# Softmax-weighted 7-tap convolution into a two-layer FFN on one core: the first block's transposed taps in two PSUM banks, and a new order of work

## The chip, the cores and the metric

One core of a Trainium2 chip runs the whole program. The metric is the device time of one execution in microseconds; lower is better. The number shown for a kernel is the median of its runs.

## The reference

For x of (4, 4096, 192) and weight_gen of (4, 4096, 8, 7), all float32:

```python
w = softmax(weight_gen, axis=-1)              # per position and head, over 7 taps
x_pad = x with 6 zero rows in front           # along the sequence
a[b, s, h, g] = sum_k w[b, s, h, k] * x_pad[b, s + k, h, g]     # 8 heads of 24 columns
u = a.reshape(16384, 192) @ w_in              # 192 x 2048
g = u * sigmoid(1.702 * u)
out = g @ w_out                               # 2048 x 192
```

The sigmoid is computed as a tanh: g = u/2 * (1 + tanh(0.851 u)).

## The kernel before, in words

The 16,384 positions are cut into 32 blocks of 512. A block's FFN is 16 units: a unit (block, f) is one [128 x 512] tile of u, that is 128 of the 2,048 hidden columns for 512 positions. Units are counted through, 0 to 15 for block 0, 16 to 31 for block 1, and so on.

**The order is written by hand.** `ORDER` (line 37) is a string of actions, one after the other, and `act` (line 755) issues the instructions of each. Since each engine and each DMA queue works through its own instructions in the order of issue, the string sets the order on every engine; semaphores between engines follow from the data. `ORDER` reaches to unit 101. From there `PERIOD` (line 22) is repeated for two blocks at a time; the change doesn't touch it.

**Block 0 is special** (`SWAP = 1`, line 383). Its products are taken in float32, since the weights are not yet split into two float16 parts by the time it starts:

- `s0.n`: the softmax of its weights (line 204).
- `ta.k` (`first_tap`, line 267): VectorE multiplies x, shifted by k, with tap k's weights, for the first 128 columns and a bit; `sum.k.l` (line 285) adds two taps on VectorE. `tb.k` and `tb.kp` (lines 301, 311) do the last 64 columns on POOL: tap by tap, then sums ("rests").
- `tr.k` (`turn_tap`, line 288): four TensorE products with the identity transpose a tap and add it in PSUM; `trb.k` (line 317) the same for the rests.
- `ka.n` (`keep_a`, line 390): copies of the two halves of the turned block to SBUF, ka.0 by ScalarE (line 396), ka.1 by VectorE (line 394). `kb.n` (line 398) are four copies of the rests, two by each (lines 405, 407).
- `W.f` (`whole`, line 541): 128 of 192 rows of the first product for unit f. `X.n` (`halves`, line 546): the remaining 64 rows, for units 4n to 4n + 3, two of them at a time in the two halves of the array. A unit is complete with both.
- `S.f` (`second`, line 577): the second product of unit f, four 128x192 pieces (`a` and `b`: two of them).
- `warm.n` (line 718): n matmuls of no use in front of all that; their result is never read.

**The weights** arrive as int64 words and are reduced in place, piece by piece: `nb` and `nm` on ScalarE, `n1` and `n2` on VectorE (line 470). Later `na`, `bin`, `bout` find their largest magnitude, and `ph`, `pl`, `ps` split them in two float16 parts (line 517); `mv` moves parts to the other half of the partitions by DMA.

**Blocks from 1 on**: softmax `s`, then `a` (`attend`, line 249): seven products and six sums on POOL. `c` (line 358) finds the block's scale with a product of one column on TensorE ("top", line 348) in the middle, `x` (line 409) splits in two float16 parts, `tu` transposes them by DMA, and `xd` copies them crosswise to the other half of the partitions, into the tile xd for odd blocks and into room in rt for even ones (line 420). `P.n` (`pair`, line 597) is the first product of units 2n and 2n + 1, 18 matmuls. P.8 is the first of block 1, P.16 the first of block 2. `gt`, `gm` (line 553) are the gate: tanh on ScalarE, a product on VectorE; `gh`, `gl` (line 570) split the result on the same two, and with them the unit's PSUM bank comes free. `U` (line 622) and `C` (line 639) are the second product, for 128 and for 64 output columns.

**PSUM**: units take the banks h0 to h3 in turn (unit mod 4, line 537). A pool tag names a bank; the turned block is in h1, the rests in h3, the second product of block 0 in o0 and o1. The scheduler puts a wait between two engines that use the same tile.

Of the kernel before, what the change touches and what calls it, by code (L numbers as in the profile page):

```python
# [38 lines left out]
tr.3 tb.1p ta.1 ta.5 tb.2 nm.t0 tb.3 sum.0.1 tb.3p nb.t0 tb.5 s1.0 trb.0 s1.1 tr.5 s1.2 n1.i0 n2.i0 s1.3 n1.t0
s1.4 tb.4 nb.i1 tb.5p tr.2 s1.5 nm.i1 n2.t0 tb.6 trb.2 s1.6 tr.0 tb.6p ka.1 ka.0 a1.0 nm.o0 W.1 a1.1 trb.4 a1.1p  # L40
kb.1 W.2 kb.0 kb.2 kb.3 n1.i1 n2.i1 W.0 X.0 nb.t1 nb.o0w n1.o0 W.3 gt.0 gt.1 nm.o1 gm.0 n2.o0 gt.2 nm.i2 a1.2
gm.1 W.4 n1.o1 a1.2p a1.3 gt.3 S.0b nb.i2w gm.2 gm.3 S.0a n2.o1 a1.3p nb.o2w W.5 X.1 W.7 W.6 n1.i2 n2.i2 s2.0
S.3 nm.i3 gt.4 s2.1 n1.i3 n2.i3 nm.t1 s3.0 a1.4 gm.4 n1.t1 nb.o4w gt.5 gm.5 a1.4p gt.7 s2.2 n2.t1 W.8 a1.5 nm.o2
W.9 n1.o2 a1.5p gt.6 s2.3 na.i2w gm.6 s2.4 nm.o4 n2.o2 gm.7 nm.o3 n1.o3 na.i0w S.2 X.2 s2.5 n2.o3 gt.8 gm.8
n1.o4 gt.9 s2.6 a1.6 gm.9 a1.6p W.10 a2.0 na.t0w W.11 n2.o4 W.12 gt.11 bin.0 W.13 a2.1 gm.11 S.4 gt.10 gm.10
na.o2w bin.1 c1.0 bin.2 S.9 na.o0w c1.1 c1.2 lp2 s5.0 a2.1p x1.0 X.3 S.6 x1.1 W.15 nm.o5 ph.i2w x1.2 s3.1 n1.o5
tu1 ph.i0w cg1 n2.o5 W.14 pl.i0w a2.2 na.o4w S.8 S.1a bout.0 gt.13 bout.1 S.10 mv.0 gm.13 a2.2p gt.14 bout.2
S.1b ph.t0w gm.14 gt.12 s5.1 pl.t0w xd1 s3.2 a2.3 ph.o4w gm.12 S.11 ph.o0w S.14b P.8 a2.3p gt.15 s5.2 gm.15
pl.i2w ph.o2w gt.17 a2.4 a2.4p s5.3 s4.0 P.9 s5.4 gt.16 gm.17 gh.17 gt.18 gm.16 gl.17 ps.o0w s3.3 gt.19 S.13
pl.o2w gm.18 gh.16 S.7 a2.5 gl.16 s3.4 gh.18 gm.19 gh.19 gl.18 s4.1 S.14a ps.o4w gl.19 S.15b P.10 s3.5 a2.5p  # L50
gt.20 P.11 pl.o0w S.5 gm.20 gt.21 gm.21 S.15a pl.o4w gh.21 gt.22 gh.20 S.12 gt.23 gl.21 a2.6 mv.1 gm.22 gl.20
U.16 gh.22 s4.2 P.12 s3.6 gm.23 ps.o2w a2.6p st.0a st.0b c2.0 gh.23 gt.24 c2.1 gl.22 s5.5 U.20 gl.23 a3.0 c2.2
x2.0 gm.24 U.18 s4.3 gt.25 x2.1 gh.24 U.21 gm.25 a3.1 gh.25 P.13 gt.26 U.17 gl.24 x2.2 U.22 gl.25 gt.27 gm.26
gm.27 U.23 P.14 a3.1p gh.26 cg2 U.24 gh.27 gl.26 gt.29 tu2 gl.27 gt.28 a3.2 co1 gm.29 gh.29 P.15 s4.4 a3.2p
gm.28 gl.29 gh.28 a3.3 U.19 gl.28 gt.31 gm.31 xd2 a3.3p U.26 gt.30 gh.31 gm.30 U.25 gh.30 gl.31 P.16 gt.32 U.31
s4.5 gl.30 gm.32 P.17 gt.33 a3.4 gm.33 U.27 a3.4p gh.32 gh.33 gt.34 s4.6 gt.35 gl.32 U.28 a3.5 gl.33 gm.34 a3.5p
a3.6 P.18 gm.35 gh.34 gl.34 a3.6p gh.35 gt.37 gt.36 gl.35 U.29 gm.37 U.30 gh.37 gm.36 c3.0 U.32 gh.36 P.19 stU.1
# [882 lines left out]
```

## Time and profile before

| | us |
|---|---|
| median of 3 runs | 1036.33 |
| lowest, highest | 1035.56, 1036.49 |
| the profiled execution | 1035.99 |
| its span | 1034.2 |
| TensorE busy in it | 1028.2 |
| VectorE, ScalarE, POOL busy | 849.6, 718.2, 729.6 |

The span is the time from the first to the last instruction of the execution that the profiler recorded; some 1.8 us of the execution lie around it. Matmuls are pipelined, so that of one can overlap the next; the start of the next says more than the duration. A float32 matmul is recorded as two rows (two passes).

### The profile page before, as it was taken

Reading aid. Unit: us, or ns where it says so; the run is one execution under the profiler, and the core shown is the slowest. Engines: PE = TensorE matmul, PEld = TensorE weight load, DVE = VectorE, ACT = ScalarE, POOL = GpSimd, SP = SyncE. Lnnn points to the kernel's source line nnn. Section 1 sums busy time; section 2 is a strip of 40 time slices with the busy share of each in tenths; the row PEclk is TensorE's granted clock in tenths of the full one; section 3 lists DMA queues with packets and bytes.
Section 4 is the critical chain, followed back from the end, with each engine's and each line's share of the span. In section 5 each row is a group of like instructions: output and inputs, shape, how many; then the busy total and the mean of one; then the engine's idle time right before and its main releaser. Section 6 shows DMA issues by size and latency. Waiting matters only on the chain.

```text
span 1034.2 us, 23101 instructions
## 1 busy us (share of the span) xinstructions
PE 1028.2 (99%) x9251; PEld 583.1 (56%) x9251; DVE 849.6 (82%) x1606; ACT 718.2 (69%) x1211; POOL 729.6 (71%) x497
## 2 busy tenths in 40 slices
...
GB/s 352 110 36 94 52 81 56 58 109 16 99 42 60 88 26 99 52 97 48 33 103 38 100 42 47 99 27 99 52 67 79 25 105 37 42 42 47 37 27 21
DMA packets 70771, 70.93 MB, mean 69 GB/s; under 512 B 51660, under 2 KB 57164, under 8 KB 69256
## 3 DMA queue, kind: packets, MB, share of 16 engines
...
q14 instruction: 35, 0.29, 0.1%
...
## 4 chain that ended last, share of the span: by engine, by line
PE 97%; DVE 1%; ACT 0%; DMA 0%; issue 0%; DVEq 0%
PE h L615 47%; PE o L634 31%; PE o L647 16%; PE o L587 2%; PE h L544 1%; PE h L550 1%; DVE tap L280 0%; DMA rt<-xt 0%; DVE row L151 0%; ACT bits L479 0%; DVE m L496 0%; PE o L672 0%; PE rest L672 0%; PE top L348 0%; DVE x L407 0%
## 5 line engine op out<-in xcount | busy, mean ns | idle before, releaser
L556 ACT ACTIVATE th<-h,s 128x512 f32<-128x512 f32 x496 | 317.0, 684 | 131.4 <-PE h L615 112.1
L561 DVE SCALAR_TENSOR_TENSOR h<-th,h 128x512 f32<-128x512 f32 x496 | 324.0, 690 | 69.2 <-ACT th L556 66.6
L261 POOL TENSOR_TENSOR acc<-acc,prod 128x768 f32<-128x768 f32 x186 | 339.4, 1825 | 13.0
L245 POOL TENSOR_TENSOR prod<-xb,wb 128x768 f32<-128x768 f32 x186 | 294.3, 1582 | 10.7
L615 PE MATMUL h<-xt,w0h 64*128 64x512 f16 x992 | 205.3, 376 | 0.0
L615 PE MATMUL h<-xt,th 64*128 64x512 f16 x496 | 183.1, 376 | 0.0
L615 PE MATMUL h<-xd,moved 64*128 64x512 f16 x768 | 156.5, 376 | 0.0
L615 PE MATMUL h<-rt,moved 64*128 64x512 f16 x720 | 149.9, 376 | 0.2 <-DMA rt<-xt 0.2
L229 POOL TENSOR_TENSOR wb<-wb,wr 128x224 f32<-128x224 f32 x31 | 18.9, 608 | 174.6 <-DVE wr L223 158.1
L615 PEld LDWEIGHTS <-moved 64*128 64x128 f16 x1488 | 96.0, 94 | 66.5
L575 DVE SCALAR_TENSOR_TENSOR g<-g,h 128x512 f16<-128x512 f16 x184 | 120.4, 681 | 7.8 <-ACT g L573 4.2
L573 ACT ACTIVATE g<-h 128x512 f16<-128x512 f32 x184 | 109.4, 597 | 25.0 <-DVE h L561 23.9
L575 DVE SCALAR_TENSOR_TENSOR ro<-ro,h 128x512 f16<-128x512 f16 x156 | 102.0, 681 | 7.3 <-ACT ro L573 4.2
L573 ACT ACTIVATE ro<-h 128x512 f16<-128x512 f32 x156 | 92.8, 597 | 20.0 <-DVE h L561 19.1
L615 PE MATMUL h<-xt,w0l 64*128 64x512 f16 x496 | 104.0, 376 | 0.0
L615 PE MATMUL h<-xd,th 64*128 64x512 f16 x256 | 96.3, 376 | 0.0
L615 PE MATMUL h<-xt,tl 64*128 64x512 f16 x248 | 93.2, 376 | 0.0
L693 ACT ACTIVATE osl<-o,s 64x512 f32<-64x512 f32 x31 | 21.1, 682 | 100.8 <-PE o L647 100.8
L615 PEld LDWEIGHTS <-w0h 64*128 64x128 f16 x992 | 63.9, 94 | 47.0 <-issue 1.4
L634 PEld LDWEIGHTS <-wos 64*128 64x128 f16 x984 | 64.0, 94 | 46.6 <-issue 0.4
L615 PE MATMUL h<-rt,th 64*128 64x512 f16 x240 | 90.2, 376 | 0.0
L615 PEld LDWEIGHTS <-th 64*128 64x128 f16 x992 | 64.1, 94 | 46.0
...
## 6 DMA issues: line engine op xcount, KB each, us to landing
...
xd<-xt SPq DMA_DIRECT2D x32, 192.0 KB, 2.9
rt<-xt SPq DMA_DIRECT2D x30, 192.0 KB, 2.9
...
```

Of the source, the lines that this page charges most:

```text
L229: eng.tensor_tensor(w, w, r, ALU.mult)
L245: eng.tensor_tensor(to.rearrange("p j (h g) -> p (j h) g", g=G), xv, wv, ALU.mult)
L261: nc.gpsimd.tensor_tensor(acc, acc, t, ALU.add)
L556: nc.scalar.activation(t, hp[u], AF.Tanh, scale=scale[u[0]][:, 4:5] if u[0] else SIG / 2)
L561: nc.vector.scalar_tensor_tensor(to, th.pop(u), 1.0, hp[u], ALU.add, ALU.mult)
L573: nc.scalar.activation(g[:, 0], hp[u], AF.Copy, scale=2.0**-12)
L575: nc.vector.scalar_tensor_tensor(g[:, 1], g[:, 0], -(2.0**12), hp.pop(u), ALU.mult, ALU.add)
L587: nc.tensor.matmul(o, lhsT=g[:, s], rhs=w, start=a and j % 2 == 0, stop=z, skip_group_check=True)
L615: nc.tensor.matmul(to, lhsT=w, rhs=x, start=i == 0, stop=i == last)
L634: nc.tensor.matmul(po[blk, e], lhsT=w[h, f * D : f * D + P], rhs=g[h, i], start=first and i == 1, stop=w is woh and n == NF - (4 if blk == ...
L647: nc.tensor.matmul(po[blk, 2][h * C1 : (h + 1) * C1], lhsT=w[:, d + P : d + D], rhs=gg[blk, f + h][:, i], start=f == 0 and i == 1, stop=f ...
L693: nc.scalar.activation(t, po[blk, 2][far_], AF.Copy, scale=s[far_, 5:6])
```

## The change

It touches four places.

- `warm`: 12 spare matmuls instead of 19.
- `turn_tap` writes the four transposed pieces of a tap into two banks, h1 and o0, two in each; `keep_a` copies one half from each. The rests go to o1 instead of h3 (`turn_rest`).
- `X.n` is now two actions, `X.na` and `X.nb`, for two units each.
- `ORDER` is written anew from its first action to unit 101.

Of the order's 46 lines the first is shown.

```diff
--- before.py
+++ after.py
@@ -35,52 +35,52 @@
...
-warm.19 s0.0 ident s0.1 s0.2 s0.3 s0.4 s0.5 s0.6 nb.i0 s0.7 nm.i0 ta.0 ta.4 tb.0 tr.4 ta.6 tr.6 ta.3 ta.2 tb.1
...
+warm.12 s0.0 s0.1 s0.2 s0.3 s0.4 s0.5 s0.6 ta.1 nm.i0 ident nb.t0 nm.t0 s0.7 tb.0 ta.0 tr.0 tr.1 tb.1 tb.1p tb.3
...
@@ -289,13 +289,13 @@
 
 
         if "a" not in turned:
-            turned["a"] = ps_h.tile([P, N], F32, tag="h1", name="tr")
+            turned["a"] = [p.tile([P, N], F32, tag=t, name="tr")[:, 0 : N // 2] for p, t in ((ps_h, "h1"), (ps_o, "o0"))]
         start, stop = not added, len(added) == len(TURNED) - 1
         added.append(k)
         for j in range(J):
             nc.tensor.matmul(
-                turned["a"][:, j * P : (j + 1) * P], lhsT=taps[k][:, j, 0:P], rhs=ident,
-                start=start and j == 0, stop=stop, skip_group_check=True,
+                turned["a"][j // 2][:, j % 2 * P : (j % 2 + 1) * P], lhsT=taps[k][:, j, 0:P], rhs=ident,
+                start=start and j % 2 == 0, stop=stop, skip_group_check=True,
             )
 
     def rest_tap(k):
@@ -318,7 +318,7 @@
 
 
         if "b" not in turned:
-            turned["b"] = ps_h.tile([P, N], F32, tag="h3", name="tr")
+            turned["b"] = ps_o.tile([P, N], F32, tag="o1", name="tr")
         i = [g[0] for g in OTHERS].index(k)
         at, start, stop = i * J * C1, not added_b, i == len(OTHERS) - 1
         added_b.append(k)
@@ -391,9 +391,9 @@
 
         h = slice(n * N // 2, (n + 1) * N // 2)
         if n:
-            nc.vector.tensor_copy(x32[0][:, h], turned["a"][:, h])
+            nc.vector.tensor_copy(x32[0][:, h], turned["a"][n])
         else:
-            nc.scalar.copy(x32[0][:, h], turned["a"][:, h])
+            nc.scalar.copy(x32[0][:, h], turned["a"][n])
 
     def keep_b(n):
 
@@ -811,13 +811,13 @@
                     bank(u)
                 whole(u, new, not new)
             elif k == "X":
-                four = units[4 * int(n) : 4 * int(n) + 4]
-                old = [u in hp for u in four]
-                for u, o in zip(four, old):
+                at = 4 * int(n[:-1]) + 2 * "ab".index(n[-1])
+                two = units[at : at + 2]
+                old = [u in hp for u in two]
+                for u, o in zip(two, old):
                     if not o:
                         bank(u)
-                for i in (0, 2):
-                    halves(four[i], four[i + 1], old[i], old[i + 1])
+                halves(*two, *old)
             elif k == "mv":
                 move(int(n))
             elif k == "P":
```

**TensorE at the start.** The rows go from the last turned taps to the first products W (L544) and X (L550, L551); tr is the turned block (L296) and the turned rests (L326), ri and rt the narrowed weights, x320 and x321 the kept block. Before:

```order
L296 MATMUL tr_204<-ident_91,tap_227 128x128 x4
L296 MATMUL tr_204<-ident_91,tap_217 128x128 x4
L326 MATMUL tr_241<-ident_91,rests_201 128x128 x2
L296 MATMUL tr_204<-ident_91,tap_197 128x128 x4
L544 MATMUL h_282<-x320_107,ri_109 128x512
L326 MATMUL tr_241<-ident_91,rests_201 128x128 x2
L544 MATMUL h_290<-x320_107,ri_109 128x512
L544 MATMUL h_297<-x320_107,ri_109 128x512
L550 MATMUL h_297<-x321_108,rt_110 128x512
L551 MATMUL h_282<-x321_108,rt_110 128x512
```

Now:

```order
L296 MATMUL tr_199<-ident_91,tap_234 128x128 x2
L296 MATMUL tr_200<-ident_91,tap_234 128x128 x2
L296 MATMUL tr_199<-ident_91,tap_232 128x128 x2
L296 MATMUL tr_200<-ident_91,tap_232 128x128 x2
L326 MATMUL tr_245<-ident_91,rests_194 128x128 x4
L544 MATMUL h_258<-x320_107,ri_109 128x512
L544 MATMUL h_260<-x320_107,ri_109 128x512
L326 MATMUL tr_245<-ident_91,rests_194 128x128 x2
L544 MATMUL h_283<-x320_107,ri_109 128x512
L550 MATMUL h_258<-x321_108,rt_110 128x512
L551 MATMUL h_260<-x321_108,rt_110 128x512
L544 MATMUL h_300<-x320_107,ri_109 128x512
```

The number behind tr is the tile: there was one, 204, for the turned block, and there are now two, 199 and 200. The first two rests stood between taps and now stand together behind all of them; the third stands behind the first two products W instead of the first one; and the first X follows the third W, with the fourth W behind it. Taps were turned in the order 4, 6, 3, 5, 2, 0 (with 1 added to it), and are now turned as 0, 1, 5, 6, 2, 3 (with 4 added to it); VectorE makes them in the order 0, 4, 6, 3, 2, 1, 5 before and 1, 0, 5, 6, 4, 3, 2 now.

**VectorE between the taps and the first gate.** L286 is the sum of two taps, L496 and L499 are n1 and n2, L209, L215 and L223 softmax steps, L394 and L407 the copies. Before:

```order
L286 TENSOR_TENSOR tap_197<-tap_197,tap_225 128x4x128
L209 TENSOR_REDUCE wm_238<-wb_117 128x32
L496 SCALAR_TENSOR_TENSOR m_195<-m_195,bits_192 128x512
L499 SCALAR_TENSOR_TENSOR ri_109<-ri_109,m_195 128x512
L215 TENSOR_REDUCE wm_238<-wb_117 128x32
L496 SCALAR_TENSOR_TENSOR m_230<-m_230,bits_235 128x512
L223 RECIPROCAL wr_239<-wm_238 128x32
L499 SCALAR_TENSOR_TENSOR rt_110<-rt_110,m_230 128x512
L394 COPY x320_107<-tr_204 128x256
L407 COPY x321_108<-tr_241 64x2x128 x2
L496 SCALAR_TENSOR_TENSOR m_264<-m_264,bits_256 128x512
```

Now:

```order
L286 TENSOR_TENSOR tap_232<-tap_232,tap_230 128x4x128
L209 TENSOR_REDUCE wm_250<-wb_117 128x32
L496 SCALAR_TENSOR_TENSOR m_182<-m_182,bits_216 128x512
L499 SCALAR_TENSOR_TENSOR ri_109<-ri_109,m_182 128x512
L394 COPY x320_107<-tr_200 128x256
L215 TENSOR_REDUCE wm_250<-wb_117 128x32
L223 RECIPROCAL wr_251<-wm_250 128x32
L496 SCALAR_TENSOR_TENSOR m_191<-m_191,bits_189 128x512
L499 SCALAR_TENSOR_TENSOR rt_110<-rt_110,m_191 128x512
L407 COPY x321_108<-tr_245 64x2x128 x2
L496 SCALAR_TENSOR_TENSOR m_269<-m_269,bits_277 128x512
```

The copy of the turned block (L394) now stands ahead of the second piece's conversion instead of behind it. Of the rests' four copies the string had kb.1, kb.0, kb.2, kb.3, taking turns between VectorE and ScalarE; it now has kb.2, kb.1 on VectorE and behind them kb.3, kb.0 on ScalarE.

**TensorE ahead of P.8.** L587 are the last products S of block 0 that come before it (g32 is the unit's gate, o the two halves of the result), L348 is a product of one column, the last row shown is P.8's first weight load. Before:

```order
L587 MATMUL o_335<-ro_111,g32_438 128x192 x2
L587 MATMUL o_344<-ro_111,g32_325 128x192 x2
L348 LDWEIGHTS ones_92
L348 MATMUL top_553<-tf_548,ones_92 128x1
L587 MATMUL o_344<-ro_111,g32_476 128x192 x2
L587 MATMUL o_335<-ro_111,g32_476 128x192 x2
L587 MATMUL o_335<-ro_111,g32_325 128x192 x2
L587 MATMUL o_344<-ro_111,g32_468 128x192 x2
L587 MATMUL o_335<-ro_111,g32_468 128x192 x2
L587 MATMUL o_335<-ro_111,g32_576 128x192 x2
L615 LDWEIGHTS w0l_94
```

Now:

```order
L587 MATMUL o_349<-ro_111,g32_295 128x192 x2
L348 LDWEIGHTS ones_92
L348 MATMUL top_587<-tf_538,ones_92 128x1
L587 MATMUL o_349<-ro_111,g32_562 128x192 x2
L587 MATMUL o_358<-ro_111,g32_562 128x192 x2
L587 MATMUL o_349<-ro_111,g32_392 128x192 x2
L587 MATMUL o_358<-ro_111,g32_392 128x192 x2
L587 MATMUL o_349<-ro_111,g32_583 128x192 x2
L587 MATMUL o_358<-ro_111,g32_583 128x192 x2
L587 MATMUL o_349<-ro_111,g32_624 128x192 x2
L615 LDWEIGHTS w0l_94
```

In both, a product S is two rows x2. Counted from W.4 on, 10.5 products S stood ahead of P.8, and now 12.5; the others follow behind it.

## Rows read from the trace of the kernel before

**Rows 1.** The page, part 1 (busy us, share of the span, instructions of TensorE and others).

```profile
PE 1028.2 (99%) x9251; PEld 583.1 (56%) x9251; DVE 849.6 (82%) x1606; ACT 718.2 (69%) x1211; POOL 729.6 (71%) x497
```

**Rows 2.** Waits of TensorE (total us, times, longest us).

```profile
PE h L544 <- ACT x L396: 1.3, 1, 1.3
...
PE h L544 <- DVE g L561: 0.3, 1, 0.3
```

**Rows 3.** Timeline of TensorE to 56 us: start, us, engine, line, work, count [idle before].

```profile
0.99 6.86 PE L722 MATMUL warm<-x 128*128 128x128 f32 x38 [0.99 <-POOL x L729]
7.68 2.84 PE L296 MATMUL tr<-ident,tap 128*128 128x128 f32 x24
...
13.04 1.06 PE L296 MATMUL tr<-ident,tap 128*128 128x128 f32 x8
15.35 1.13 PE L544 MATMUL h<-x,ri 128*128 128x512 f32 x2 [1.25 <-ACT x L396]
16.32 0.61 PE L326 MATMUL tr<-ident,rests 128*128 128x128 f32 x4
16.77 1.89 PE L544 MATMUL h<-x,ri 128*128 128x512 f32 x4
18.59 0.70 PE L550 MATMUL h<-x,rt 64*128 64x512 f32 x1
...
20.68 1.13 PE L544 MATMUL h<-x,ri 128*128 128x512 f32 x2
22.14 1.13 PE L544 MATMUL h<-x,ri 128*128 128x512 f32 x2 [0.33 <-DVE g L561]
...
42.01 0.16 PE L348 MATMUL top<-tf,ones 128*128 128x1 bf16 x1
...
49.27 4.32 PE L587 MATMUL o<-ro,g 128*128 128x192 f32 x24
53.53 0.39 PE L615 MATMUL h<-xt,w0l 64*128 64x512 f16 x2
...
55.48 0.38 PE L615 MATMUL h<-xt,w0l 64*128 64x512 f16 x2
```

**Rows 4.** The same timeline of VectorE.

```profile
5.84 4.74 DVE L280 TENSOR_TENSOR tap<-xb,w 128x576 f32<-128x576 f32 x7
...
17.04 0.43 DVE L407 COPY x<-tr 64x256 f32<-64x256 f32 x1 [2.14 <-PE tr L326]
...
21.40 0.69 DVE L561 SCALAR_TENSOR_TENSOR g<-th,h 128x512 f32<-128x512 f32 x1
...
46.63 1.28 DVE L526 SCALAR_TENSOR_TENSOR w0l<-ri,sc,w0h 128x1024 f16<-128x1024 f32 x1
```

**Rows 5.** The same timeline of ScalarE.

```profile
17.49 0.36 ACT L405 COPY x<-tr 64x256 f32<-64x256 f32 x1 [1.66 <-DVE x L407]
...
20.77 1.08 ACT L556 ACTIVATE th<-h 128x512 f32<-128x512 f32 x2
```

**Rows 6.** The same timeline of SyncE's DMA queue, 50 to 330 us.

```profile
49.97 1.19 SPq L430 DMA_DIRECT2D xd<-xt  x2
...
80.70 1.13 SPq L430 DMA_DIRECT2D rt<-xt  x2
```

**Rows 7.** DMA issues (count, KB each, us to landing), and products of tile rt.

```profile
xd<-xt SPq DMA_DIRECT2D x32, 192.0 KB, 2.9
...
L615 PE MATMUL h<-rt,moved x192: 376/376/376, 84.5 to 296.6; 64*128 64x512 f16 x192
```

**Rows 8.** The timeline of POOL.

```profile
27.70 0.57 POOL L211 TENSOR_TENSOR wb<-wb,wm 128x224 f32<-128x224 f32 x1
...
37.37 1.83 POOL L261 TENSOR_TENSOR acc<-acc,prod 128x768 f32<-128x768 f32 x1
```

**Rows 9.** Stretches, spare matmuls alone: TensorE busy us (count), weight loads, granted clock, DMA.

```profile
3.20:5.20 2.00, 2.00 (x11) 2.00 (x10) 1.00 1.00 382
6.20:7.20 1.00, 1.00 (x11) 1.00 (x10) 1.00 1.05 430
```

More of the change, by code (lines that the diff above doesn't have):

```diff
@@ L37 @@
 ORDER = """
-warm.19 s0.0 ident s0.1 s0.2 s0.3 s0.4 s0.5 s0.6 nb.i0 s0.7 nm.i0 ta.0 ta.4 tb.0 tr.4 ta.6 tr.6 ta.3 ta.2 tb.1
[L39 to L57, printed above, removed]
@@ L83 @@
-gl.100 x7.0 cg7 gl.101
+warm.12 s0.0 s0.1 s0.2 s0.3 s0.4 s0.5 s0.6 ta.1 nm.i0 ident nb.t0 nm.t0 s0.7 tb.0 ta.0 tr.0 tr.1 tb.1 tb.1p tb.3
+tb.2 tb.3p tb.5 tb.4 nb.i0 ta.5 tr.5 ta.6 tr.6 ta.4 ta.3 ta.2 tr.2 sum.3.4 tr.3 trb.0 trb.2 s1.0 s1.1 n1.i0
+n2.i0 ka.0 ka.1 W.0 W.1 tb.5p tb.6 tb.6p s1.2 s1.3 s1.4 s1.5 nm.i1 n1.t0 n2.t0 trb.4 kb.2 kb.1 nb.i1 n1.i1 n2.i1
+kb.3 kb.0 W.3 nm.o0 X.0a gt.0 gm.0 gt.1 gm.1 nb.o0w n1.o0 W.2 X.0b gt.3 gm.3 gt.2 gm.2 nm.o1 n2.o0 W.4 nb.i2w
+s1.6 a1.0 W.5 X.1a X.1b nm.i2 n1.o1 n2.o1 n1.i2 W.7 n2.i2 gt.4 gm.4 nb.o2w nm.i3 n1.i3 nm.t1 W.6 S.0a a1.1 a1.1p
```

66 lines of the change are left out of this document (41 added, 25 removed).

## The prediction

> **What bounds the kernel now.** I read the page first. TensorE is busy for 1028.2 of 1034.2 us [rows 1], so a microsecond is to be had only where it is idle or where its work is cut, and all that the change cuts is spare matmuls. The waits come next: 1.3 us for ScalarE's copy at line 396 and 0.3 us for VectorE's gate at line 561 [rows 2]; both lie in the first 23 us. So I read the timeline of TensorE from its start to P.8, the first product of the steady kind [rows 3], and then, engine by engine, what it waits for there.
>
> The reader should see this in it [rows 3]. Warm-up matmuls run until 7.6. The six turned taps and two of the three rests fill 7.68 to 14.10 without a gap. Then TensorE does nothing until W.1 at 15.35: VectorE copies one half of the turned block, and only then ScalarE the other. From 20.68 to 22.14 it does one W, which is 0.86 us of work (two are 1.72 at 16.77, from 16.77 to 18.49); the other 0.6 us are a wait for a gate.
>
> **The change, part by part**, in times of TensorE's timeline:
>
> 1. *Taps turned.* VectorE's seven taps start at 5.84, one every 0.665 us, 0.75 us each [rows 4]. Before, tap 4 came second; now it is tap 0, over at 7.25 as tap 4 was, and with no spare matmul in front of it the first transpose starts some 0.15 later, at 7.40 instead of 7.68. Transposes start every 0.112 us (24 from 7.68 to 10.36 [rows 3]), so 48 take 5.36. Their order is now the one in which taps are made: tap 2 is ready at 10.58 and wanted at 10.97, the sum of 3 and 4 ready at 11.24 and wanted at 11.87. No gap, end at 12.76; eight transposes of rests, 0.90, end at 13.66. Seven spare matmuls less thus gain 0.28 and no more, because the taps are next in line.
>
> 2. *Two banks.* VectorE's copy starts after the last tap has drained, at about 13.05, and takes 0.41 (a copy of this kind is 0.43 [rows 4]); ScalarE's reads the other bank and starts before it. Both are over at 13.5, under the rests. W.0 starts at 13.66 instead of 15.35: **1.69 us gained here**.
>
> 3. *The copies of the rests.* The third rest moves behind W.0 and W.1: 13.66 + 1.72, with the switch 15.5, and 0.61 with its drain [rows 3], so 16.1. POOL, which had it ready before 16.32, has it sooner, since a softmax step now stands behind it. The rests still share one bank. Before, VectorE and ScalarE took turns for four copies, 17.04 to 18.7. Now VectorE does two and ScalarE two behind them: 16.2, + 0.35 + 0.43 [rows 4], + 0.29 + 0.36 [rows 5] and the handovers: X.0a at 17.7. TensorE has W.3 to do meanwhile, until 16.8, so **0.9 us of new idle** opens, where before W.2 and W.0 filled the time. For the same work done it is 17.7 against 18.59.
>
> 4. *The 64-row products in two steps.* Four halves took 2.09 (18.59 to 20.68 [rows 3]), two are 1.05: X.0a to 18.75, W.2 to 19.65, X.0b to 20.7, where W.4 may start. What the split buys: units 0 and 1 are complete at 18.8; two tanh, 1.08 [rows 5], and a first gate of 0.69 [rows 4] beside the second tanh free the bank at 20.1. The 0.6 us wait is gone: 20.7 against 22.14, **1.44 us**. What the split costs, one more switch, is in these numbers.
>
> 5. *From W.4 to P.8* stand the same W and X, but 12.5 instead of 10.5 products S. One S is 1.42 (three from 49.27 to 53.53 [rows 3]). P.8 moves to 53.53 - 1.44 + 2.84 = 54.93; the two S are missing behind it, so this is no loss. P.8 needs xd, which was just in time before: it is issued in two parts from 49.97, the second at 50.6 and landing 2.9 later at 53.5 [rows 6, 7]. That hangs on TensorE's one-column product at 42.01, 11.5 us earlier [rows 3]. Ahead of this product stand one W less and 2.5 S more, counted from W.4: 20.7 + 19.87 - 0.86 + 3.55 = 43.26, and xd lands at 54.75. Its input is there: POOL's sum for block 1 ended at 39.2 [rows 8] and now has one more softmax step of 0.57 ahead of it, less 0.1 for its sooner start; what VectorE then does with it fitted before 42.01 and fits before 43.26. Cover 0.2 us: **no wait, barely**.
>
> 6. *P.16.* Its rt is issued from 80.70 in two parts and lands at 84.1, and is wanted at 84.5 [rows 6, 7]. One U more stands ahead now (six matmuls at 1.95/18 us, as from 53.53 to 55.48: 0.65): wanted at 84.5 - 1.44 + 0.65 = 83.7. POOL's sum for block 2 ends when it did, as the step that block 1 gained is taken from block 2. So rt lands between 83.7 and 84.1; bounds of the wait 0 and 0.4, and I take **0.2**, the middle.
>
> Behind P.16 the order differs in detail, not in work, and TensorE had no wait there that it names; nothing is added. Sum: -1.44 + 0.2 = -1.24 us. The profiled execution took 1035.99, so 1034.75 with a span near 1033.0. The median of the runs shown is 0.34 above that execution; against it, **1035.1**.
>
> **The clock.** The spare matmuls are slow at first: 11 passes touch the 2 us from 3.2 to 5.2, and 11 touch the one from 6.2 to 7.2 [rows 9]; apart 0.213 us, then 0.112. That is the step from 1.2 to 2.4 GHz, after work without a break since 0.99, though the granted clock reads 1.00 in both rows. Twelve spare matmuls last until about 6.0, where the step had just come; 1.4 us of idle follow, which are new. The 1.25 us of idle ahead of 15.35 left the clock high, so I take it as high at 7.40. The Trainium skill, page "TensorE: Matmul & The Clock Gate", section on the HAM clock gate, speaks against the change: there the clock is low by default, activity releases it, and the same kernel has more or fewer slow matmuls from run to run. By that rule some executions would turn the taps at the low clock and come out as in the first rival; by the row none.
>
> **Rivals.**
>
> *The taps are turned at the low clock* (chance 0.10). With as many slow passes as the spare matmuls had, 22, each 0.101 longer: 2.2 us. -1.24 + 2.2 = +1.0: **1037.3**, slower. For it: the spare matmuls end close behind the step. Against it: idle of the same length did no harm. It decides from the point where the last spare matmul ends before the step.
>
> *The transfers of blocks 1 and 2 set the pace* (0.15). VectorE has more ahead of block 1's scale: one gate less, but two conversions and three softmax steps more, 1.5 us, where it had idle of as much before. If half of that shows in xd and rt, P.8 and P.16 wait 0.9 together instead of 0.2: -0.5, **1035.8**.
>
> *The rests' copies overlap* (0.15). If ScalarE's two need only one of VectorE's, X.0a comes 0.4 sooner; with 0.3 off elsewhere and no wait at P.16, -2.1: **1034.2**. Against it: two copies of one bank never ran together before (17.04, then 17.49 [rows 4, 5]).
>
> *The S are missed behind P.8* (0.08). There 3.5 instead of 5.5 are left between the first pairs. A pair is 1.95 on TensorE; VectorE's four passes for it are 0.69 each, 2.8, and in between come conversions of 1.28 [rows 4]. If all 2.84 us of moved cover become idle: -1.24 + 2.84 = +1.6, **1037.9**, slower. It decides where a gate frees its bank only after TensorE asks for it.
>
> **How the numbers follow.** Forecast 0.52 (its own range 1034.6 to 1035.6), rivals 0.48. A measurement of this kernel can tell about 0.2% from no change, 2.07 us: faster is below 1034.3, slower above 1038.4. More than half of the overlapping case and the lower edge of the forecast lie below: 0.18. Of the two slow cases a part lies above, where one comes with half of another: 0.07. The rest, 0.75, is within. The range takes in the overlapping case less 0.5, by which the runs differ among themselves, and the first slow case: 1033.7 to 1037.2.
>
> **What would show it.** The first tap's product at 7.4; W.0 near 13.7 with no idle of TensorE between the transposes and it; both copies of the tap block side by side; 0.9 us of idle ahead of X.0a at 17.7; W.4 near 20.7 without a wait for a gate; P.8 near 54.9; a wait for rt at P.16 under 0.5. A step of the clock behind 7.4, a gap over 0.5 us ahead of P.8, or waits for gates between P.9 and P.13 would prove it wrong.

## The result and the profile after

The changed kernel takes 1041.37 us in the median (1040.89 to 1042.07), the kernel before on the same chip 1036.15: a ratio of 1.0051, 95% interval 1.0038 to 1.0064. It is slower by 5.2 us. The forecast was 1.2 us faster; the time lies outside the range. The profiled execution took 1040.89 us, with a span of 1039.1.

The page of the changed kernel, part 1, against [rows 1]: TensorE's work is the same but for the spare matmuls, and VectorE is busy for 6 us more with as many instructions.

```profile
PE 1028.5 (99%) x9237; PEld 577.5 (56%) x9237; DVE 855.5 (82%) x1606; ACT 718.8 (69%) x1211; POOL 730.3 (70%) x497
```

The waits of TensorE in the changed kernel, against [rows 2] (total us, times, longest us). The copy at line 396 and the early gate are gone from the list. The idle ahead of the transposes (1.6) and of X.0a (1.0) is new, as forecast; so are waits for transfers (xd, rt) and for VectorE's gates and splits (lines 561, 575).

```profile
PE tr L296 <- DVE tap L280: 1.6, 1, 1.6
PE h L550 <- ACT x L405: 1.0, 1, 1.0
...
PE h L615 <- DMA xd<-xt: 0.9, 3, 0.4
PE h L615 <- DVE g L575: 0.9, 1, 0.9
PE h L615 <- DMA rt<-xt: 0.6, 2, 0.5
PE o L634 <- DVE ro L575: 0.6, 1, 0.6
```

The timeline of TensorE in the changed kernel, against [rows 3]: W.0 at 13.73 for 15.35, X.0a at 17.94, W.4 at 21.14 for 22.14. The start came as forecast. The one-column product (line 348) on which xd hangs is at 43.54. P.8 begins at 55.99 with more S done ahead of it, the last of them behind a wait of 0.36 us for a gate, and stops twice for xd.

```profile
0.99 4.83 PE L722 MATMUL warm<-x 128*128 128x128 f32 x24 [0.99 <-POOL x L729]
7.41 5.60 PE L296 MATMUL tr<-ident,tap 128*128 128x128 f32 x48 [1.59 <-DVE tap L280]
...
13.73 1.89 PE L544 MATMUL h<-x,ri 128*128 128x512 f32 x4
...
17.94 0.70 PE L550 MATMUL h<-x,rt 64*128 64x512 f32 x1 [1.01 <-ACT x L405]
...
21.14 1.99 PE L544 MATMUL h<-x,ri 128*128 128x512 f32 x4
...
43.54 0.17 PE L348 MATMUL top<-tf,ones 128*128 128x1 bf16 x1
...
55.11 0.94 PE L587 MATMUL o<-ro,g 128*128 128x192 f32 x4 [0.36 <-DVE g L561]
55.99 0.39 PE L615 MATMUL h<-xt,w0l 64*128 64x512 f16 x2
56.68 0.37 PE L615 MATMUL h<-xd,moved 64*128 64x512 f16 x1 [0.30 <-DMA xd<-xt]
57.48 0.37 PE L615 MATMUL h<-xd,moved 64*128 64x512 f16 x1 [0.43 <-DMA xd<-xt]
```

**A ledger of the time.** For each pair P.n I take its start less that in the kernel before, and subtract the TensorE work that one order has ahead of P.n and the other has not (each matmul at what its undisturbed neighbours take, so to some 0.1 us). What is left is lateness at equal work: -1.0 us at W.4, -0.26 at P.8, +0.81 at P.9, +1.0 at P.10 to P.14, +2.07 at P.15, +2.72 at P.17, +3.68 at P.22, +4.08 at P.25, +4.54 at P.41, +5.14 from P.53 to P.176. At the end of the span it is 4.9, since the kernel before loses some tenths late too. So 4.3 of the 6.1 us lost behind W.4 go between P.8 and P.25, in a few steps with nothing between them. At most of them the timeline names a wait for xd, for rt or for VectorE; the largest behind P.9 are at P.15, inside P.16 and ahead of P.22:

```profile
83.13 0.39 PE L615 MATMUL h<-xt,w0l 64*128 64x512 f16 x2 [0.90 <-DVE g L575]
88.08 0.37 PE L615 MATMUL h<-rt,moved 64*128 64x512 f16 x1 [0.46 <-DMA rt<-xt]
108.04 0.39 PE L634 MATMUL o<-ro,wos 64*128 64x512 f16 x2 [0.60 <-DVE ro L575]
```

**What made VectorE late.** Its timeline in the changed kernel: the scale of a block (line 362), the two passes xs that split the block (line 416) and the float16 splits of the weights (line 526).

```profile
41.09 0.95 DVE L362 TENSOR_REDUCE top<-acc 128x1 f32<-128x768 f32 x1
...
45.58 3.62 DVE L416 SCALAR_TENSOR_TENSOR xs<-acc,s,xs 128x512 f16<-128x512 f32 x2
...
54.98 1.96 DVE L526 SCALAR_TENSOR_TENSOR wol<-ro,sc,woh 128x1024 f16<-128x1024 f32 x1
...
57.72 1.97 DVE L526 SCALAR_TENSOR_TENSOR wol<-ro,sc,woh 128x1024 f16<-128x1024 f32 x1
...
73.10 0.94 DVE L362 TENSOR_REDUCE top<-acc 128x1 f32<-128x768 f32 x1
...
77.75 2.77 DVE L416 SCALAR_TENSOR_TENSOR xs<-acc,s,xs 128x512 f16<-128x512 f32 x2
```

The same lines in the kernel before:

```profile
39.90 0.94 DVE L362 TENSOR_REDUCE top<-acc 128x1 f32<-128x768 f32 x1
...
43.84 1.51 DVE L416 SCALAR_TENSOR_TENSOR xs<-acc,s,xs 128x512 f16<-128x512 f32 x2 [0.58 <-ACT xs L413]
...
58.69 1.28 DVE L526 SCALAR_TENSOR_TENSOR wol<-ro,sc,woh 128x1024 f16<-128x1024 f32 x1
...
74.04 0.87 DVE L416 SCALAR_TENSOR_TENSOR xs<-acc,s,xs 128x512 f16<-128x512 f32 x1
...
76.03 0.57 DVE L416 SCALAR_TENSOR_TENSOR xs<-acc,s,xs 128x256 f16<-128x256 f32 x1
```

The passes are the same in size and number (an x2 of xs is one of 512 columns and one of 256; the row prints the size of the first); they are longer. Two passes xs take 3.62 us instead of 1.51, with no idle time marked ahead of them. POOL's timeline in the changed kernel tells why: its product and its sums follow one another without a break while xs is at work, and its passes grow too (a sum is 1.83 us in [rows 8]).

```profile
45.15 1.55 POOL L245 TENSOR_TENSOR prod<-xb,wb 128x768 f32<-128x768 f32 x1
46.78 2.14 POOL L261 TENSOR_TENSOR acc<-acc,prod 128x768 f32<-128x768 f32 x1
49.00 1.61 POOL L245 TENSOR_TENSOR prod<-xb,wb 128x768 f32<-128x768 f32 x1
```

The first pass of xs ends up behind the product, the second behind the sum, which ends at 48.92; xs ends at 49.20. That is 3.85 us later than before: 1.74 because the new order begins it later, 2.11 because it takes longer. Then xd is issued at 53.83 instead of 49.97 [rows 6], and P.8 waits.

So there is one more number to follow, the **excess**: what the passes of lines 416 and 526 between 40 and 130 us take beyond 0.575 us for a pass of xs and 1.28 for a split, which is what they take where POOL is still (below). It is 1.36 us before and 7.33 after, to some 0.2 us, as passes that follow one another overlap in the rows. It goes along with the time in the table below, but it can't tell by itself whether long passes make a kernel late or lateness makes passes long; runs 3 and 6 change POOL and can.

### The profile page after: what moved, and what is told of

The parts are those of the page before. It is cut to its first block, busy times and chain, and to the rows that moved or that the text cites. A ratio compares the mean times of both kernels' runs of the same rounds, so it can differ in the third digit from the quotient of the medians.

```text
span 1039.1 us, 23077 instructions
## 1 busy us (share of the span) xinstructions
PE 1028.5 (99%) x9237; PEld 577.5 (56%) x9237; DVE 855.5 (82%) x1606; ACT 718.8 (69%) x1211; POOL 730.3 (70%) x497
## 4 chain that ended last, share of the span: by engine, by line
PE 92%; DVE 4%; DMA 2%; ACT 1%; issue 1%; SPq 0%; ACTq 0%; DVEq 0%
PE h L615 44%; PE o L634 28%; PE o L647 16%; PE o L587 1%; PE h L544 1%; DMA xd<-xt 1%; DVE xs L416 1%; DMA xt<-xs 1%; DVE h L561 1%; DMA rt<-xt 1%; PE h L550 1%; PE tr L296 1%; DVE g L575 1%; ACT th L556 0%; ACT ro L573 0%
## 5 line engine op out<-in xcount | busy, mean ns | idle before, releaser
L634 PEld LDWEIGHTS <-woh 64*128 64x128 f16 x984 | 62.8, 94 | 46.3
```

Source lines behind the costliest of these rows:

```text
L634: nc.tensor.matmul(po[blk, e], lhsT=w[h, f * D : f * D + P], rhs=g[h, i], start=first and i == 1, stop=w is woh and n == NF - (4 if blk == ...
```

## The experiments

In the expectations "xs and the splits" are lines 416 and 526. In those from the fifth run on, theory 1 is that VectorE's passes with two operands in SBUF and POOL's passes stretch each other, and that the new order brings more of them together; theory 2 is that the new order is late on VectorE by itself. The first four number their theories as they say. Of long lines of `ORDER` the diffs show only the part around the edit.

| run | median us | before, same chip | ratio, 95% interval | span of its profile | excess |
|---|---|---|---|---|---|
| kernel before | | 1036.15 | | 1034.2 | 1.36 |
| the change | 1041.37 | 1036.15 | 1.0038 to 1.0064 | 1039.1 | 7.33 |
| 1 new start, old order | 1040.02 | 1036.12 | 1.0024 to 1.0049 | 1038.7 | 4.38 |
| 2 old start, new order | 1040.77 | 1036.12 | 1.0031 to 1.0061 | 1038.7 | 7.73 |
| 3 POOL held for xs | 1041.05 | 1036.12 | 1.0033 to 1.0060 | 1039.1 | 6.35 |
| 4 two banks alone | 1035.59 | 1036.12 | 0.9987 to 1.0005 | 1034.8 | 2.04 |
| 5 before, short POOL passes | 1037.27 | 1036.05 | 1.0003 to 1.0022 | 1035.2 | 0.72 |
| 6 change, short POOL passes | 1037.15 | 1036.05 | 1.0001 to 1.0019 | 1034.7 | 0.35 |
| 7 change to P.11 | 1039.46 | 1036.05 | 1.0022 to 1.0046 | 1037.1 | 4.68 |
| 8 new start, 19 spare | 1035.68 | 1036.05 | 0.9989 to 1.0008 | 1034.7 | 1.46 |
| 9 before, start late | 1036.64 | 1035.82 | 0.9997 to 1.0016 | 1035.5 | 1.44 |
| 10 before, POOL late | 1036.93 | 1035.82 | 0.9999 to 1.0018 | 1035.8 | 2.81 |
| 11 change, 19 spare | 1040.56 | 1035.82 | 1.0030 to 1.0060 | 1038.7 | 7.50 |
| 12 change from P.26 on | 1036.83 | 1035.82 | 1.0002 to 1.0021 | 1034.9 | 1.86 |
| 13 new start, 16 spare | 1036.22 | 1035.76 | 0.9994 to 1.0013 | 1035.0 | 1.80 |
| 14 new start, 22 spare | 1036.92 | 1035.76 | 1.0001 to 1.0020 | 1034.1 | 1.91 |
| 15 new start, 12 spare | 1040.02 | 1035.79 | 1.0026 to 1.0054 | 1039.8 | 5.17 |
| 16 new start, 14 spare | 1036.57 | 1035.79 | 1.0001 to 1.0022 | 1038.3 | 4.82 |

No row with an excess under 3 has a span above 1036, and none with more has one under 1037. The excess and the span belong to one profiled execution, the median to all.

**Which part loses: runs 1, 2 and 4.** Run 1 has the change's order up to X.0b (with its 12 spare steps) and the order of before behind it.

```diff
-W.3 nm.o0 X.0a gt.0 gm.0 gt.1 gm.1 nb.o0w n1.o0 W.2 X.0b gt.3 gm.3 gt.2 gm.2
+W.3 nm.o0 X.0a gt.0 gm.0 gt.1 gm.1 nb.o0w n1.o0 W.2 X.0b s1.6 a1.0 a1.1 a1.1p
```

> The change's start (12 spare matmuls, two banks, taps in the new order, both X in two steps) up to X.0b, and behind it the order of before. Theory 1, the loss is in the new order behind W.4: W.4 near 21.1 as in the changed kernel, 1.0 us sooner than before; P.8 then waits for block 1's xd, which POOL's sum holds, so 0.4 to 1.0 of it is left at the end: 1035.1 to 1035.8. Rival, a sooner start by itself brings VectorE and POOL into each other's way: 1038 or more, with VectorE's two passes of xs for block 1 near 3.6 us.

Run 2 has before's start with 19 spare steps, one bank, and the change's order behind X.0.

```diff
-warm.12 s0.0 s0.1 s0.2 s0.3 s0.4 s0.5 s0.6 ta.1 nm.i0 ident nb.t0
+warm.19 s0.0 ident s0.1 s0.2 s0.3 s0.4 s0.5 s0.6 nb.i0 s0.7 nm.i0 ta.0
```

> The start of before (19 spare matmuls, one bank for the turned block, the old order) up to X.0b, and behind it the change's order. Theory 1: the order alone loses about 6 us against before: 1041 to 1042.5. Rival, the order is harmless and only the sooner start upsets it: 1036 to 1038.

Run 4 is the kernel before with the two banks and the two steps of X, one right behind the other.

```diff
-            turned["a"] = ps_h.tile([P, N], F32, tag="h1", name="tr")
+            turned["a"] = [p.tile([P, N], F32, tag=t, name="tr")[:, 0 : N // 2] for p, t in ((ps_h, "h1"), (ps_o, "o0"))]
...
-X.0
+X.0a X.0b
```

> Before, with its order and 19 spare matmuls, and only the two banks for the turned block (and X in two steps next to each other). Theory 1: ScalarE's copy no longer waits for VectorE's, W.1 near 14.95 instead of 15.35; at the end 0.0 to 0.4 less than before: 1035.8 to 1036.2. Rival, banks matter little as VectorE's own queue holds its copy until 14.5: W.1 at 15.3 and no difference.

Measured: the new order alone loses 4.6 us; its ledger has the steps of the changed kernel (+1.46 at P.9, +2.71 at P.15, +4.32 at P.22). The two banks cost nothing: run 4 has W.1 at 15.02, 0.33 us sooner, and its time can't be told from before's. Run 1 loses 3.9 us with before's order. Its theory 1 had none of that; its rival had the time, but with xs of block 1 near 3.6 us, and xs took 1.47. Runs 8 and 13 to 16 come back to it.

**Is it the meeting of xs with POOL: run 3.** The changed kernel; POOL waits, through a copy of 8 columns, until xs of block 1 is done, and the eight POOL steps that stood ahead of it follow.

```diff
-x1.0 x1.1 x1.2 tu1
+x1.0 x1.1 x1.2 hx a2.2 a2.2p a2.3 a2.3p a2.4 a2.4p s5.1 a2.5 tu1
...
+            elif k == "hx":
+                nc.gpsimd.tensor_copy(held, xs[1][:, 0, 2 * D - 8 : 2 * D])
```

> The changed kernel, with POOL made to wait for VectorE's two passes of xs for block 1 (a copy of 8 columns of xs on POOL; eight of POOL's steps stand behind it). Theory 1a, these passes take 3.6 us because each stands behind a pass of POOL: they take 1.2 to 1.6, TensorE has no wait for xd inside P.8 (1.07 us in the changed kernel), and of that 0.5 to 1.0 is left at the end: 1040.4 to 1040.9; POOL is later by 1.5, so P.16 may give some of it back. Rival 1b, the passes are slow for a reason of their own: still over 3 us, same time as the changed kernel or more.

The timeline of VectorE in run 3 (its line 414 is line 416 of before, 524 is 526):

```profile
45.55 1.15 DVE L414 SCALAR_TENSOR_TENSOR xs<-acc,s,xs 128x512 f16<-128x512 f32 x2
...
48.66 2.57 DVE L524 SCALAR_TENSOR_TENSOR w0l<-ri,sc,w0h 128x1024 f16<-128x1024 f32 x1
...
76.99 2.69 DVE L414 SCALAR_TENSOR_TENSOR xs<-acc,s,xs 128x512 f16<-128x512 f32 x2
```

With POOL still, xs takes 1.15 us for 3.62, and the loss at P.8 and P.9 goes: the ledger stands at -0.24 from P.10 to P.14. But POOL's passes, now later, meet the splits: the first takes 2.57, and xs of block 2 is as long as ever. At P.15 the ledger is at +1.24, at P.22 at +3.37, and the time is not better. One meeting was moved, not removed.

**All meetings gone: runs 5 and 6.** POOL's products and sums of taps 1 to 6 in blocks 2 to 5 are cut from 768 columns to 24, in before's order (5) and in the change's (6). The sums of these blocks are left incomplete.

```diff
-                tap(blk, nc.gpsimd, t, k, w)
+                n = D if not 2 <= blk <= 5 else G
+                if n == D:
+                    tap(blk, nc.gpsimd, t, k, w)
+                else:
+                    nc.gpsimd.tensor_tensor(t[:, 0, 0:n], xb[i][:, jb * J + k, 0:n], w[:, 0:1, k].to_broadcast([P, n]), ALU.mult)
...
```

> The kernel before, with POOL's products and sums for taps 1 to 6 of blocks 2 to 5 cut from 768 columns to 24 (the sums of these blocks are then incomplete; every instruction and every wait stays, each pass is only short). It is the base for the next run. Both theories: nearly the time of before, 1034.5 to 1036.5 us, since the kernel before has few waits for POOL; VectorE's passes xs of blocks 1 and 2 take 1.15 us each and the float16 splits 1.28 each, as where POOL is still.

> The changed kernel with the same cut of POOL's passes. Theory 1 (VectorE loses its time because its passes with two operands in SBUF run against POOL's, and the new order brings more of them together): xs takes 1.15 us in blocks 1 and 2, VectorE is in time at P.8 and P.15, the gain of the start is kept, and the time is 0.5 to 1.2 us below that of the run with before's order and short passes. Theory 2 (the new order itself puts the passes of block 2, from the scale on, behind more gates and splits on VectorE, clash or no clash): xs takes 1.15 us, but the waits for VectorE at P.15 and P.22 and for rt behind P.16 remain, and the time stays 2.5 to 5 us above the run with before's order and short passes.

VectorE's timeline in run 6 (line 420 is 416, 530 is 526):

```profile
45.55 1.32 DVE L420 SCALAR_TENSOR_TENSOR xs<-acc,s,xs 128x512 f16<-128x512 f32 x2
48.67 1.27 DVE L530 SCALAR_TENSOR_TENSOR w0l<-ri,sc,w0h 128x1024 f16<-128x1024 f32 x1
...
53.30 1.28 DVE L530 SCALAR_TENSOR_TENSOR wol<-ro,sc,woh 128x1024 f16<-128x1024 f32 x1
...
75.87 1.14 DVE L420 SCALAR_TENSOR_TENSOR xs<-acc,s,xs 128x512 f16<-128x512 f32 x2
```

The changed kernel loses 4.2 of its 5.2 us (1041.37 to 1037.15), and behind the start TensorE waits for VectorE for 0.3 us in all. Shorter POOL passes could also act by delivering sooner, but between 40 and 130 us no wait of VectorE or ScalarE for POOL is listed in the kernel before, in the changed kernel or in runs 2, 5 and 6. Theory 2 had 2.5 to 5 us left above run 5, with the waits at P.15 and P.22; neither came, and as the main cause it falls. Theory 1 stands, though its 0.5 to 1.2 us of gain did not come.

That the change is now 0.1 us below before's order (1037.15 against 1037.27) says less than it seems, since run 5 has a loss of its own. It was not expected. Its SyncE queue issues rt of block 2 at 82.47 instead of 80.70 [rows 6], and its ledger against the kernel before goes from +0.09 to +1.34 at P.16:

```profile
82.47 1.13 SPq L434 DMA_DIRECT2D rt<-xt  x2
```

```profile
PE h L619 <- DMA rt<-xt: 0.9, 2, 0.5
```

The ledger of run 6 against the kernel before goes from -0.9 at P.14 to +1.20 at P.53, where the change goes from +1.0 to +5.14. So of the 6.1 us that the change loses behind W.4, 3.9 go with POOL's long passes of blocks 2 to 5, and 2.2 stay: 0.4 at P.16 (rt), 0.6 at P.25, 0.6 from P.40 to P.43, 0.44 at P.53 and some tenths between (run 12 has more on the last).

**Where in the order: runs 7 and 12.** Run 7 keeps the change, with POOL held as in run 3, to the end of P.11, and has before's order from P.12 on. Run 12 has run 8's kernel to P.25 and the change's order from P.26 on.

```diff
-mv.1 P.12 st.0b gt.25 gt.24 c2.0 gm.25 gh.25
+mv.1 P.12 st.0b c2.0 gt.24 c2.1 s5.5 U.20 c2.2 x2.0
```

> The changed kernel to the end of P.11 with POOL held until xs of block 1 is done (as in the third run), and before's order from P.12 on. If what is lost at P.15 and later comes from the new order of the steps behind P.12 (theory 2, or theory 1 with the clash of block 2 in it): the lead of 0.2 us that the third run had at P.10 to P.14 is kept to the end, xs of block 2 takes 1.4 to 1.5 us as before, and the time is 1035.3 to 1036.3 us. If VectorE is already behind by then from what came before P.12 (splits that clash with POOL, 3 us longer in the third run than alone), the waits at P.15 and P.17 come in before's order too: 1038 to 1040 us.

> The eighth run's kernel (the change's start with 19 steps, before's order) to P.25, and the change's order from P.26 on. If the 1.0 us that the changed kernel still loses at P.41, P.43 and P.53 is in the order of these steps: 1036.5 to 1036.9 us. If it is only what VectorE and POOL were behind by then: 1035.4 to 1036.0 us, as the eighth run.

Run 7 loses 3.4 us, the time of the second answer, but not by its waits: by P.12 VectorE has 3.1 us of excess (before 1.1), and the main wait that follows is TensorE's for the scale of block 2, ahead of P.13, which before's order asks for sooner.

```profile
PE top L348 <- DVE tf L344: 2.1, 1, 2.1
```

Run 12 is 1.0 us above before and, over the ratios, some 1.2 above run 8, whose interval its own just overlaps: its ledger rises by 0.5 us from P.27 to P.30 and by 0.43 at P.53. So about 1 us of the loss is in the late part of the order. The step at P.53 is in the change and in runs 6 and 12, and it is a meeting again: the last pass of xs of block 7 begins while a product of POOL is under way and ends behind it. VectorE and POOL in the changed kernel:

```profile
229.22 1.22 DVE L416 SCALAR_TENSOR_TENSOR xs<-acc,s,xs 128x256 f16<-128x256 f32 x1
```

```profile
228.62 1.54 POOL L245 TENSOR_TENSOR acc<-xb,wb 128x768 f32<-128x768 f32 x1
```

In the kernel before the same pass takes 0.48 us at 224.44, with POOL idle. Behind it TensorE waits 0.25 us for a split of VectorE at 231.09. Run 6 shortened blocks 2 to 5 alone and has the long pass too (1.23 us). What costs the rest of the late part, no run shows.

**The start and the number of spare matmuls: runs 8, 11, 13 to 16.** Run 8 is run 1 with 19 steps, 13 with 16, 14 with 22, 15 with 12 again, 16 with 14. Run 11 is the changed kernel with 19.

```diff
-warm.12 s0.0 s0.1 s0.2
+warm.19 s0.0 s0.1 s0.2
```

> The first run again (the change's start to X.0b, before's order behind) with 19 steps of spare matmuls instead of 12. The first run fell in clock (granted 0.73 at 5 to 10 us) after 2.1 us of idle time ahead of the transposes. If the low clock made its loss: granted clock 1.00 throughout, transposes begin no later than 7.7 us, W.0 at 14.0, and the time is 1035.0 to 1036.3. If before's order can't use a sooner start (phases shift and passes clash), the clock is full and the time still 1038 or more.

> The changed kernel with 19 steps of spare matmuls, and nothing else: its transposes begin at 8.04 instead of 7.41 us, as in the eighth run, and TensorE and VectorE come 0.6 us later against POOL. Theory 1: the excess of xs and the splits changes with the phase (7.3 us in the changed kernel), and the time follows it; if the first pass of xs still meets a POOL sum, 1040.5 to 1042.5 us; if it falls clear, 1037 to 1039 us. Rival (the order loses on its own, phase or not): 1041.8 to 1042.2 us, 0.6 us above the changed kernel, with the waits at P.8, P.15, P.17, P.22 and P.25 as there.

> The eighth run's kernel (the change's start, before's order behind) with 16 steps of spare matmuls instead of 19: they end at about 7.1 us, the transposes begin with the second tap at 7.4 instead of 8.04. If the loss of the first run (12 steps) came from the low clock of its transposes and what followed from 1 us of delay: the clock stays at 1.00, W.0 is at 13.7, P.8 at 53.3 to 53.6, and the time is 1035.0 to 1036.0 us. If a start sooner than the eighth run's makes VectorE and POOL meet: above 1038 us with an excess of xs and the splits above 3 us.

> The same with 22 steps: the transposes begin 1.05 us later than in the eighth run at the full clock, so that P.8 comes near 54.9 us as in the first run, without its low clock. If 1 us of lateness is enough for block 1's transfers and for VectorE to fall among POOL's passes: 1038.5 to 1040.5 us, with xd late at P.8 and an excess of 3 us or more behind it. If the lateness alone costs what it is: 1036.5 to 1037.0 us, xd in time, excess near 1.5 us; the first run's loss then needed the low clock or something else of its own.

> The first run's kernel again (12 steps of spare matmuls, the change's start, before's order behind), for a second profile of it. If the first run's 1040 us needs the fallen clock of its profiled execution: another profile in which TensorE is idle 1.6 us ahead of the transposes and the clock stays at 1.00 has P.8 at 53.4 to 53.6 us and about 1036 us like the run with 16 steps, and slow executions of it have a clock below 1. If 12 steps lose without it: 1039.5 to 1040.5 us with the clock at 1.00, and the ledger of that profile shows at which step.

> The same with 14 steps, two less than the run with 16 (1036.2 us). If idle time ahead of the transposes is what costs, it lies between the two: 1036 to 1038 us with some executions near 1036 and some near 1040. If not, 1036.2 us as with 16.

With 16, 19 and 22 steps the new start under before's order comes out at 0.4 us below to 1.2 above before. The time at W.0 doesn't reach the end. Run 11, the change with 19 steps, loses 4.7 us with an excess of 7.50: xs took 3.57 us, as its expectation had for that case, so the change's own loss does not come from its 12 steps. In run 13 W.0 is at 13.73 as in the change, W.4 at 21.13, and then S.0 waits, which stood right behind W.4 at 23.11 before; P.8 is at 53.44, 0.09 sooner than before. TensorE's timeline in run 13:

```profile
13.73 1.89 PE L544 MATMUL h<-x,ri 128*128 128x512 f32 x4
...
21.13 1.13 PE L544 MATMUL h<-x,ri 128*128 128x512 f32 x2
22.89 1.60 PE L587 MATMUL o<-ro,g 128*128 128x192 f32 x8 [0.62 <-issue]
```

With 12 steps it loses 4 us, again in run 15. Its profile shows the clock: the spare matmuls end at 5.3, TensorE is idle for 2.11 us, and the transposes run at a granted clock that falls to 0.73 in the stretch from 5 to 10 us (a timeline row, and the stretches).

```profile
7.41 7.17 PE L296 MATMUL tr<-ident,tap 128*128 128x128 f32 x48 [2.11 <-DVE tap L280]
```

```profile
5.00:10.00 5.00, 2.89 (x15) 2.73 (x14) 4.91 (x9) 1.33 (x3) 4.16 (x7) 0.73 1.03 410
10.00:15.00 5.00, 5.00 (x44) 5.00 (x44) 3.21 (x7) 1.99 (x5) 4.76 (x7) 0.93 1.05 393
```

They take 7.17 us for 5.60. But the fallen clock seems not to be needed: three of the five executions of run 15 and four of the five of run 1 had a mean granted clock of 1.00, and took 1039.15 to 1040.46 all the same. (A mean of 1.00 does not exclude slow transposes: the slow spare matmuls of [rows 9] read 1.00 too.) Run 16 shows a way without it. Two of its ten executions took 1040.1 us and the other eight 1035.3 to 1036.8, as its first case had it, and the profiled one took 1040.1, with a granted clock of 1.00 and 5.59 us for the transposes. Up to xs it is run 13 (xs at 43.68 in both), and the first instruction behind that differs by more than 0.15 us is the transposing DMA, SyncE's queue in run 16,

```profile
45.55 2.53 SPq L422 DMA_TRANSPOSE xt<-xs  x1
```

and in run 13:

```profile
45.52 1.59 SPq L422 DMA_TRANSPOSE xt<-xs  x1
```

takes 0.9 us longer to issue. xd is issued 0.85 later, P.8 waits 0.8 us for it, and VectorE comes 0.9 us later to the next split. VectorE and POOL of run 16 at that place:

```profile
59.60 2.00 DVE L526 SCALAR_TENSOR_TENSOR wol<-ro,sc,woh 128x1024 f16<-128x1024 f32 x1
```

```profile
58.99 1.54 POOL L245 TENSOR_TENSOR prod<-xb,wb 128x768 f32<-128x768 f32 x1
```

and POOL in the kernel before, beside the split of 1.28 us at 58.69 that was shown above:

```profile
58.88 2.49 POOL L245 TENSOR_TENSOR prod<-xb,wb 128x768 f32<-128x768 f32 x1
```

Before, VectorE is first by 0.2 us, keeps its time, and POOL's product takes 0.95 longer. In run 16 POOL is first and keeps its time, and VectorE's split takes 0.72 longer. Everything behind it on VectorE is later by that, and the next splits (2.19 at 67.63) and xs of block 2 (2.06 at 76.61) meet POOL from behind too: excess 4.8 us, span 1038.3. So 0.8 us of lateness at P.8 became 4. In runs 1 and 15 the xd transfers were slow to issue (2.07 and 2.12 us for 1.19), and the same followed; but both profiles were late before that, run 15 by 1.6 us at W.0 and by 2.7 behind xs. No run shows why a DMA takes longer to issue in some executions, nor why all ten executions with 12 steps were long.

**How small a shift is enough: runs 9 and 10.** The kernel before with 22 spare steps, and the kernel before with POOL's passes from block 2 on moved by five small copies (1.20 us).

```diff
-warm.19 s0.0 ident s0.1
+warm.22 s0.0 ident s0.1
...
-a1.6p W.10 a2.0
+a1.6p W.10 dl.5 a2.0
...
+            elif k == "dl": [nc.gpsimd.tensor_copy(held, ident[:, 0:8]) for _ in range(int(n))]
```

> The kernel before, with 22 steps of spare matmuls instead of 19 and nothing else: at 0.18 us a matmul (6.7 us for 38) its transposes, and with them TensorE and VectorE, come some 1.05 us later, while POOL's sums of block 2 don't wait for either. Theory 1 (the phase of VectorE against POOL at 43 to 80 us decides, and 1 us in it is enough, as between the first run and the eighth): xs and the splits together take 2.5 to 4.5 us longer than alone (1.4 us before), VectorE comes late at P.12 to P.17, and the time is 1039 to 1041 us. Rival (a late start costs what it is late): 1037.0 to 1037.4 us, and xs and the splits as before.

> The kernel before, with five copies of 8 columns on POOL ahead of the first product of block 2, so that POOL's passes from there on come 0.8 to 0.9 us later and nothing else moves. POOL is idle for 3 us before 106 us, so late sums alone cost nothing. Rival (POOL has room): 1035.5 to 1036.5 us. Theory 1: the overlaps of POOL's passes with xs and the splits change, so their excess changes, either way: by it the time should be above before's by what the excess is above 1.4 us, one for one within 1 us.

Run 9 was to move TensorE and VectorE by 1.05 us and moved P.8 by 0.59, since the waits at W.1 and W.4 took up the rest; POOL followed. The excess stayed at 1.44 and the time rose by 0.8: the expected 3 to 5 us did not come, and this size of shift is not enough. Run 14 was to test 1 us and did not, as its spare matmuls ran faster and its P.8 was at 53.44. In run 10 the excess is 2.81, 1.45 more than before, of which 1.16 is xs of block 1, and the time 1.1 more, though POOL alone was moved. That is what theory 1 had, within its 1 us. It is weak by itself: the interval just takes in no change, and 0.37 us of the lateness in its profile stands at W.4, ahead of the copies.

## Why the prediction was wrong

- **Steps 1 to 3 held.** First transpose 7.41 (forecast 7.40), W.0 13.73 (13.66), X.0a 17.94 (17.7) behind 1.01 us of idle (0.9).
- **Step 4, in part.** W.4 is at 21.14, not 20.7: a gain of 1.00, not 1.44.
- **Step 5 failed** at the way from the one-column product to xd, "11.5 us earlier", which was carried over at the length that it had, with VectorE's passes at the durations that they had. The product itself came at 43.54 (forecast 43.26). P.8's last wait for xd ended at 57.48, 13.9 us behind it, where the forecast had xd landed at 54.75: xs took 3.62 us instead of 1.51. "Cover 0.2 us: no wait, barely" became 1.07 us between P.8 and P.9. Ahead of P.8 0.7 us of the gain at W.4 were already gone, about half of it the wait for a gate at 55.11.
- **Step 6 and the sentence behind it failed**: rt was to cost 0.2 us (at most 0.4) and cost 0.6, and "Behind P.16 the order differs in detail, not in work, and TensorE had no wait there that it names; nothing is added" put the rest at nothing. P.15, which no step of the prediction priced, P.17, P.22 and P.25 cost 3.1 us in the ledger with the 0.6 of rt in it, P.41 to P.53 1.1. VectorE, busy for 21.59 of the 22 us from 58 to 80 in the kernel before, had no slack for 6 us of excess. An engine that is nowhere waited for can be a fraction of a microsecond from it.
- **The rivals.** "The transfers of blocks 1 and 2 set the pace" names where the first waits came; it priced VectorE's lateness by the steps ahead of xs and not by xs itself, at 0.9 us for xd and rt together. They cost 1.7 in the ledger (1.07 at P.8, 0.63 at P.16), and VectorE's own gates and splits cost more than that behind them. The slow case with S missing behind P.8 did not come: there was no wait for gates from P.10 to P.14.
- **The clock.** In the changed kernel it stayed at 1.00 in all six executions, as the forecast took it. With the same spare matmuls and before's order it fell in the profiles of runs 1 and 15, behind idle times of 2.13 and 2.11 us, and not behind 1.59 or 1.31. The price was 1.6 us (7.17 less 5.60), the rival had 2.2. The rule that the prediction cited from the Trainium skill, page "TensorE: Matmul & The Clock Gate", agrees with these two runs, as a thing of single executions (two of run 15's five have a mean granted clock of 0.998, three of 1.00); it does not make the 5.2 us.

The cause of the 5.2 us is thus shown as far as this: with POOL's long passes of blocks 2 to 5 the new order alone loses 4.6 us (run 2), without them the changed kernel loses 4.2 us less (run 6), with POOL held xs is short again (run 3), and the excess tells the long executions from the short ones in all rows of the table. Open are 1.7 of the 6.1 us lost behind W.4, which run 6 keeps and no meeting was found for. The Trainium skill, page "SBUF — State Buffer", section "Who interferes with whom", has a rule for such meetings: a VectorE instruction with two inputs in SBUF and a GpSimd instruction that reads SBUF exclude each other for their whole length (GpSimd is POOL here), the one that issued first goes on, and with one input in SBUF there is no conflict. The trace agrees: lines 416 and 526 read two tiles in SBUF and are stretched, to 1.8 us for a pass of xs (3.62 for two); the gates and splits of g (lines 561, 575) read one operand from PSUM and take 0.62 to 0.70 in all these kernels. The trace of the kernel before had a row to see it by: a sum of POOL beside VectorE's split of [rows 4] is 2.78 us long, not 1.83 as in [rows 8].

```profile
46.83 2.78 POOL L261 TENSOR_TENSOR acc<-acc,prod 128x768 f32<-128x768 f32 x1
```
